# Two weight-folding matmuls and a sparse attention on one core: loads in 1 MB pieces, and batch 0 ahead of the fold

## The chip, the cores and the metric

The kernel runs on one core of a Trainium2 chip. The metric is the device time of one execution in microseconds. The kernel before the change took 296.65 us, the median of 13 runs between 292.83 and 298.26.

The engines are TensorE (PE, with its weight loads PEld), VectorE (DVE), ScalarE (ACT), GpSimd (POOL) and SyncE (SP). Each takes its instructions in the order in which the program was laid out for it. SP issues all loads, ACT issues the stores of the output, POOL makes most of the casts from fp32 to fp16.

## The reference

```python
# 8 batches, 8 heads, 576 tokens, head size 64
scores = (q @ k.T) / 8
mask_local   = (rel >= 0) & (rel < 32)                    # heads 0 to 3
mask_strided = (rel >= 0) & (col % 32 == row % 32)        # heads 4 to 7
x = softmax(where(mask, scores, -1e9)) @ v                # to (4608, 512)
a, b = x @ w1, x @ w2                                     # 512 -> 1024
out = ((a * b) @ w3) @ w_out                              # 1024 -> 1024 -> 512
```

Inputs and output are fp32: q, k and v of 9.4 MB each, w1, w2 and w_out of 2 MB, w3 of 4 MB; the output has 9.4 MB.

## The kernel before

**Fold.** No nonlinear step stands between w3 and w_out, so the kernel first computes w34 = w3 @ w_out (1024 x 512) once. For each of 8 row blocks of w3, `fold_tr` transposes the fp16 block on TensorE and copies the result to `w3T` (one half by DVE, one by ACT), and `fold_mm` multiplies it with `woh`, the fp16 w_out, in two halves of four matmuls, the second of which evicts the sum to `w34`. The row blocks in fp16 (`w3n`) have four buffers.

**Attention.** Each batch has four pairs of heads: two local, two strided. A pair goes through the steps `ph_T` (transposes of q and k, copied from PSUM to `qT`, `kT`), `ph_S` (scores, then exp on ACT to `pte` and the product with a mask on DVE to `ptm`), `ph_PV` (twice: product with v, reciprocal of the sums, and the scaled product `xqs`) and `ph_T2` (transposes of the result, copied to `xT`). `ph_R`, once a batch, transposes the last 64 tokens of q and k. The scores and the PV results share a PSUM pool of two buffers (`psB`), the transposes have a pool of one (`psM`). In batches 0 and 1 (`b < AHEAD`) ACT makes all copies of `ph_T` and `ph_R`; later DVE makes those of k.

**Feed-forward.** The 4608 tokens are taken in 9 chunks of 512. `ab_halves` gives 16 units (8 for a, 8 for b; four matmuls of 512 columns each; ACT copies a out of PSUM, DVE multiplies it with b to `abt`). `o_halves` gives 8 units with w34, and stores four blocks of output.

**Order.** It is written out by hand. All attention steps stand in one list, `stream`. `host(units, upto, lead)` lays out units one after the other and, after each, as many steps of the list as bring it evenly to `upto`. `pe(...)` holds the matmuls in this order. Before, the fold hosts batch 0, ab of chunk 0 hosts 8 steps of batch 1 (the first nine units none), o of chunk 0 the other 17, and each later chunk hosts the next batch. Stream steps run one batch ahead of the chunk that needs them.

**Loads.** Each `load_*` helper takes a staging buffer from `stgp` (nine of 0.5 MB), issues DMAs on SP and casts on POOL (w1 on ACT). A batch has q and k in two groups of four heads (packets of 1 KB), their last 64 tokens (`load_rest`, 256 B), local v (`load_vL`, 256 B) to partitions 32 to 127, from where DVE copies to the low ones, and strided v (`load_vS`, 2 KB). A load waits for its staging buffer's last cast, and a cast for the buffer that it writes. The weights are mixed with batch 0: w3 and w_out first, then w1 and w2 in quarters, then batch 1.

Of the kernel before, what the change touches and what calls it, by code (L numbers as in the profile page):

```python
# [8 lines left out]
FP32 = mybir.dt.float32  # L9
FP16 = mybir.dt.float16  # L10
# [4 lines left out]
def _ap(t: bass.AP, off_add, dims):  # L15
    return bass.AP(tensor=t.tensor, offset=t.offset + off_add, ap=dims)
# [3 lines left out]
def kernel(  # L20
# [27 lines left out]
    LQ, LT = 96, 6  # L48
# [3 lines left out]
    KW = 640  # L52

    consts = ctx.enter_context(tc.tile_pool(name="consts", bufs=1))
    stgp = ctx.enter_context(tc.tile_pool(name="stgp", bufs=9))
    qkp = ctx.enter_context(tc.tile_pool(name="qkp", bufs=2))
    att = ctx.enter_context(tc.tile_pool(name="att", bufs=2))
    ffn = ctx.enter_context(tc.tile_pool(name="ffn", bufs=2))
# [6 lines left out]
    def pe(ins):  # L65
        return tc.keep_in_program_order(ins)

    def copy(eng, out, in_):
        if eng == "a":
            nc.scalar.copy(out=out, in_=in_)  # L70
        elif eng == "v":
            nc.vector.tensor_copy(out=out, in_=in_)  # L72
        else:
            nc.gpsimd.tensor_copy(out=out, in_=in_)  # L74
# [55 lines left out]
    w3T = [ffn.tile([P, KF // 2, DF], FP16, tag="abt", bufs=4, name=f"w3T{i}") for i in range(2)]  # L130
    w3n = {}

    def load_wo(g, eng):
        src = moe_w_out.rearrange("(c p) n -> p c n", p=P)
        st = stgp.tile([P, 2, DM], FP32, tag="stg")
        nc.sync.dma_start(st, src[:, 2 * g:2 * g + 2, :])
        copy(eng, woh[:, 2 * g:2 * g + 2, :], st)

    def load_w3(jc, eng):
        st = stgp.tile([P, DF], FP32, tag="stg")  # L140
        nc.sync.dma_start(st, moe_w3[bass.ds(jc * P, P), :])
        t = ffn.tile([P, DF], FP16, tag="w3n", bufs=4)
        w3n[jc] = t
        copy(eng, t, st)

    def load_w12(g):
        cs = bass.ds(g * 256, 256)
        for wd, wh, eng in ((moe_w1, w1h, "a"), (moe_w2, w2h, "p")):
            st = stgp.tile([P, KM, 256], FP32, tag="stg")
            nc.sync.dma_start(st, wd.rearrange("(c p) n -> p c n", p=P)[:, :, cs])  # L150
            copy(eng, wh[:, :, cs], st)


    x16 = {}

    def load_qk(b, grp, engs="pp"):
        for nm, ten, eng in (("q", q, engs[0]), ("k", k, engs[1])):
            st = stgp.tile([P, 4, 4, D], FP32, tag="stg")
            nc.sync.dma_start(st.rearrange("p h c d -> p h (c d)"),
                              ten[b, 4 * grp:4 * grp + 4, 0:NM].rearrange("h (p c) d -> p h (c d)", c=4))  # L160
            t = qkp.tile([P, 4, 4, D], FP16, tag=f"{nm}{grp}")
            copy(eng, t, st.rearrange("p h c d -> p c h d"))
            x16[(b, nm, grp)] = t

    def load_rest(b, eng="p"):
        st = stgp.tile([P, H, D], FP32, tag="stg")
        for i, ten in enumerate((q, k)):
            nc.sync.dma_start(st[64 * i:64 * i + 64], ten[b, :, NM:S].rearrange("h p d -> p h d"))
        t = qkp.tile([P, H, D], FP16, tag="r")
        copy(eng, t, st)  # L170
        x16[(b, "r")] = t

    def load_vL(b):
        vt = v16L[b % 2]
        for hp in range(2):
            hs = slice(2 * hp, 2 * hp + 2)
            st = stgp.tile([P, 2, LT, D], FP32, tag="stg")
            for h in range(2):
                nc.sync.dma_start(st[32:P, h], v[b, 2 * hp + h].rearrange("(t p) d -> p t d", p=LQ))  # L179
            for pr in (bass.ds(32, 32), bass.ds(64, 64)):  # L180
                nc.gpsimd.tensor_copy(out=vt[pr, hs, :, 0:D], in_=st[pr])  # L181
            nc.vector.tensor_copy(out=vt[0:32, hs, 1:LT, 0:D], in_=vt[96:P, hs, 0:LT - 1, 0:D])

    def load_vS(b):
        vt = v16S[b % 2]
        for hp in range(2):
            st = stgp.tile([SQ, 2, ST, D], FP32, tag="stg")
            sf = st.rearrange("p h c d -> p h (c d)")
            sv = v[b, 4 + 2 * hp:6 + 2 * hp].rearrange("h (p c) d -> p h (c d)", c=ST)
            nc.sync.dma_start(sf[0:64], sv[0:64])  # L190
            nc.sync.dma_start(sf[64:SQ], sv[64:SQ])
            nc.gpsimd.tensor_copy(out=vt[:, 2 * hp:2 * hp + 2, :, 0:D], in_=st)  # L192


    class Pair:
# [101 lines left out]
    def ab_halves(tch):  # L297
        tok = bass.ds(tch * NT, NT)
        res = []

        def first():
            abts[tch] = ffn.tile([P, KF, NT], FP16, tag="abt", bufs=4, name=f"abt{tch}")

        for jc in range(KF):
            st = {}

            def a(jc=jc, st=st):
                if jc == 0:
                    first()
                aps = psF.tile([P, NT], FP32, tag="f")  # L310
                for ci in range(KM):
                    pe(nc.tensor.matmul(aps, w1h[:, ci, bass.ds(jc * P, P)], xT[ci][:, tok],  # L312
                                        start=(ci == 0), stop=(ci == KM - 1)))
# [12 lines left out]
        return res  # L326
# [84 lines left out]
    load_w3(0, "p")  # L411
    for g in range(4):
        load_wo(g, "p")
    load_w3(1, "p")
    load_qk(0, 0)
    load_rest(0)
    load_w3(2, "p")
    load_vL(0)
    load_w3(3, "p")
    load_qk(0, 1)  # L420
    load_w3(4, "p")
    load_w3(5, "p")
    load_vS(0)
    load_w3(6, "p")
    load_w3(7, "p")
    load_w12(0)
    load_w12(1)
    load_w12(2)
    load_qk(1, 0)
    load_rest(1)  # L430
    load_w12(3)
    load_vL(1)
    load_qk(1, 1)
    load_vS(1)

    fold = []
    fold_tr(0)
# [6 lines left out]
    host(fold, batch_end[0], lead=3)  # L444
    load_qk(2, 0)
    load_rest(2)
    load_vL(2)
    host(ab_halves(0), pos[0] + 8, lead=9)
    load_qk(2, 1)
    load_vS(2)  # L450
    host(o_halves(0), batch_end[1])
    for tch in range(1, NTILE):
        units = ab_halves(tch) + o_halves(tch)
        if tch + 1 < B:
            more = tch + 2 < B
            if more:
                load_qk(tch + 2, 0)
                load_rest(tch + 2)
                load_vL(tch + 2)
            mid = (pos[0] + batch_end[tch + 1]) // 2  # L460
            host(units[0:12], mid)
            if more:
                load_qk(tch + 2, 1)
                load_vS(tch + 2)
            host(units[12:], batch_end[tch + 1])
        else:
            for u in units:
                u()
# [30 lines left out]
```

The softmax here doesn't subtract the row's maximum and nothing guards it: scores larger than these inputs give would overflow.

## Time and profile before

| What | Value |
|---|---|
| Median of 13 runs | 296.65 us |
| The profiled execution | 297.62 us, its span 295.9 us |
| Busy in the span: PE, PEld, DVE, ACT, POOL | 268.2, 141.9, 169.9, 146.7, 102.3 us |
| DMA | 48.64 MB, 163 GB/s over the span |
| Bytes moved, 14 to 22 us and 22 to 30 us | 181 and 344 GB/s |
| Cast of 128 x 1024 on POOL, on ACT | 1074 (median 1040), 1048 ns |
| exp of 128 x 576, of 72 x 576 on ACT | 657, 644 ns |
| mask product on DVE, local, strided | 612, 571 ns |
| reciprocal and product on DVE, local | 182 + 554 ns |
| reciprocal and product on DVE, strided | 199 + 685 ns |

The busy times are shares of the whole span; the matmuls' own times overlap, since they are pipelined. The execution falls into three parts: a head of some 84 us, in which the weights and the first batches come in, six stages of 28 us (a chunk hosting a batch each), and two chunks without attention of 20.7 us each at the end.

### The profile page before, as it was taken

To read this page: it belongs to the slowest core of one execution; us is meant where nothing else is said; L and a number is where in the kernel's file an instruction comes from. 1 tells how busy PE (TensorE), PEld (TensorE's weight loads), DVE (VectorE), ACT (ScalarE), POOL (GpSimd) and SP (SyncE) were. 2 spreads that over 40 slices of the span, in tenths; PEclk is the share of its full clock that TensorE was granted. 3 is DMA by queue.
4 is the path that set the end of the run, shared out by engine and by line. 5 is a ranking of instruction groups with operands and counts; after the bars stand their busy time and mean duration, and the time that the engine had idled before them with its cause. 6 is when DMAs were issued, how large, how long until landed. Compare 5 with 4: busy or idle time off the path is not lost.

```text
span 295.9 us, 6132 instructions
## 1 busy us (share of the span) xinstructions
PE 268.2 (91%) x2401; PEld 141.9 (48%) x2401; DVE 169.9 (57%) x353; ACT 146.7 (50%) x269; POOL 102.3 (35%) x118
## 2 busy tenths in 40 slices
PE   2349998987979999999999999999999999999995
PEld 1115554444545555555555455555554555444442
DVE  2012864364878865896788479657755774330420
ACT  2025596556655465546554644555465545323332
POOL 5638643366746634753456435110000000000000
PEclk9986999999999999999999999999999999999999
DMA  7999999899969948995997692120021002003003
GB/s 235 360 180 352 290 348 243 158 252 212 293 205 231 271 114 256 277 167 181 270 232 198 201 278 45 38 106 2 2 73 73 0 2 106 35 2 134 8 2 142
DMA packets 58653, 48.64 MB, mean 164 GB/s; under 512 B 29184, under 2 KB 49664, under 8 KB 58624
## 3 DMA queue, kind: packets, MB, share of 16 engines
q1 hardware_dynamic: 53440, 38.81, 54.5%
q10 hardware_dynamic: 5184, 9.44, 8.8%
q8 instruction: 19, 0.31, 0.5%
q14 instruction: 10, 0.08, 0.1%
HBM read 38.80 MB, written 9.44 MB: 163 GB/s over the span
## 4 chain that ended last, share of the span: by engine, by line
PE 64%; DMA 21%; ACT 5%; DVE 2%; issue 2%; SPq 2%; POOL 1%; ACTq 0%
PE bps L321 18%; PE ops L335 18%; PE aps L312 17%; DMA st<-in_moe_w_dram 10%; DMA st<-in_k_dram 6%; PE xps L268 4%; PE ps L214 3%; DMA st<-in_moe_w_out_dram 3%; DMA out_dram<-osb 3%; PE sps L248 2%; ACT pte L253 2%; PE ps L284 2%; ACT xT L291 1%; SPq L179 1%; ACT osb L346 1%
## 5 line engine op out<-in xcount | busy, mean ns | idle before, releaser
L312 PE MATMUL aps<-xT,w1h 128*128 128x512 f16 x288 | 75.3, 379 | 2.5 <-ACT xT L291 2.4
L323 DVE TENSOR_TENSOR abt<-bps,asb 128x512 f16<-128x512 f32 x72 | 49.5, 687 | 47.1 <-PE bps L321 45.4
L321 PE MATMUL bps<-xT,w2h 128*128 128x512 f16 x288 | 74.0, 379 | 0.0
L315 ACT COPY asb<-aps 128x512 f32<-128x512 f32 x72 | 42.2, 586 | 63.9 <-PE aps L312 61.1
L335 PE MATMUL ops<-w,abt 128*128 128x512 f16 x288 | 71.5, 379 | 0.0
L74 POOL CAST t<-st 128x1024 f16<-128x1024 f32 (+1 forms) x48 | 47.7, 998 | 37.9 <-DMA st<-in_k_dram 24.6
L253 ACT ACTIVATE pte<-sps 128x576 f16<-128x576 f32 (+1 forms) x64 | 38.4, 650 | 8.2 <-PE sps L248 7.1
L276 DVE TENSOR_TENSOR xqs<-xps,rcp 96x384 f16<-96x384 f32 (+1 forms) x64 | 39.6, 619 | 2.0
L321 PEld LDWEIGHTS <-w2h 128*128 128x128 f16 x288 | 25.8, 97 | 30.9 <-issue 4.8
L70 ACT COPY qT<-ps 128x512 f16<-128x512 f16 (+1 forms) x48 | 22.9, 481 | 29.0 <-PE ps L214 22.6
L312 PEld LDWEIGHTS <-w1h 128*128 128x128 f16 x288 | 25.1, 98 | 22.2
L335 PEld LDWEIGHTS <-abt 128*128 128x128 f16 x288 | 24.7, 98 | 22.2
L346 ACT COPY osb<-ops 128x512 f32<-128x512 f32 x36 | 21.1, 586 | 27.7 <-PE ops L335 27.7
L181 POOL CAST v16L<-st 32x768 f16<-32x768 f32 (+1 forms) x32 | 26.9, 840 | 20.0 <-PE xps L268 10.7
L268 PEld LDWEIGHTS <-ptm 72*128 72x128 f16 (+1 forms) x448 | 21.6, 97 | 18.3 <-DVE ptm L255 5.7
L255 DVE TENSOR_TENSOR ptm<-pte,maskL 128x576 f16<-128x576 f16 x32 | 19.4, 612 | 12.8 <-ACT pte L253 12.3
L72 DVE COPY kT<-ps 128x512 f16<-128x512 f16 (+1 forms) x36 | 18.8, 535 | 9.7 <-ACT qT L70 9.6
L192 POOL CAST v16S<-st 72x1024 f16<-72x1024 f32 x16 | 17.1, 1074 | 20.6 <-PE xps L268 12.9
L255 DVE TENSOR_TENSOR ptm<-pte,maskS 72x576 f16<-72x576 f16 x32 | 18.1, 571 | 8.4 <-ACT pte L253 7.8
L335 PE MATMUL ops<-woh,w3T 128*128 128x512 f16 x64 | 19.8, 439 | 2.2 <-POOL woh L74 1.5
L214 PEld LDWEIGHTS <-t 128*128 128x128 f16 x256 | 17.1, 99 | 9.3 <-issue 2.6
L214 PE MATMUL ps<-id,t 128*128 128x128 f16 x256 | 20.3, 222 | 0.8 <-POOL t L74 0.8
(48 smaller groups left out, 173.2 us busy)
## 6 DMA issues: line engine op xcount, KB each, us to landing
out_dram<-osb ACTq DMA_DIRECT2D x36, 256.0 KB, 2.0
st<-in_moe_w_dram SPq DMA_DIRECT2D x16, 512.0 KB, 9.4
st<-in_q_dram SPq DMA_DIRECT2D x16, 512.0 KB, 5.4
st<-in_k_dram SPq DMA_DIRECT2D x16, 512.0 KB, 5.7
st<-in_v_dram SPq DMA_DIRECT2D x32, 144.0 KB, 5.7
st<-in_v_dram SPq DMA_DIRECT2D x16, 256.0 KB, 7.6
st<-in_moe_w_out_dram SPq DMA_DIRECT2D x4, 512.0 KB, 7.4
st<-in_q_dram SPq DMA_DIRECT2D x8, 128.0 KB, 7.1
```

Of the source, the lines that this page charges most:

```text
L74: nc.gpsimd.tensor_copy(out=out, in_=in_)
L181: nc.gpsimd.tensor_copy(out=vt[pr, hs, :, 0:D], in_=st[pr])
L214: pe(nc.tensor.transpose(ps[:, i, c * P:(c + 1) * P], src[:, c, h0:h0 + 2].rearrange("p h d -> p (h d)"), id16))
L253: nc.scalar.activation(out=pte[0:kr], in_=sps[0:kr, :, 0:288], func=AF.Exp, bias=0.0, scale=scale)
L255: nc.vector.tensor_mul(ptm[0:kr, 0:576].rearrange("p (a x) -> p a x", x=w), pte[0:kr].rearrange("p h (a x) -> p (h a) x", x=w), _ap(mk, 0, ...
L268: pe(nc.tensor.matmul(xps[:, h, i * 65:(i + 1) * 65], ptm[0:kr, c0:c0 + P], vt[0:kr, 2 * (s.hp % 2) + h, g * m + i, :], start=True, stop=T ...
L276: nc.vector.tensor_mul(xqs[0:w, 0:m].rearrange("p i h d -> p h i d"), xv[:, :, :, 0:D], _ap(rcp, 0, [[rp, w], [4, 2], [1, m], [0, D]]))
L312: pe(nc.tensor.matmul(aps, w1h[:, ci, bass.ds(jc * P, P)], xT[ci][:, tok], start=(ci == 0), stop=(ci == KM - 1)))
L315: nc.scalar.copy(out=asb, in_=aps)
L321: pe(nc.tensor.matmul(bps, w2h[:, ci, bass.ds(jc * P, P)], xT[ci][:, tok], start=(ci == 0), stop=(ci == KM - 1)))
L323: nc.vector.tensor_mul(abts[tch][:, jc, :], bps, st["asb"])
L335: pe(nc.tensor.matmul(st["ps"], lhs(ci), rhs(ci), start=(ci == 0), stop=(ci == KF - 1)))
```

## The change

- The staging pool has five buffers of 1 MB in place of nine of 0.5 MB; `load_rest` has a buffer of its own.
- q and k of all heads come in one DMA each, local v in one, strided v in one of 64 partitions and one of 8; w1 and w2 come in halves of 512 columns, w_out in halves, w3 in four pairs of row blocks. Casts keep their sizes, except local v's, of which there are two per batch in place of four. Of each half of w_out one cast is on POOL and one on ACT; of batch 0, k's casts are on ACT; of w3, the second row block's.
- Order of the loads: batch 0, w1 and w2, the first pair of w3, w_out, the rest of w3, batch 1.
- The stream's steps of batch 0 stand alone, each after a `spin`: two matmuls of the identity whose result nobody reads.
- Then ab of chunk 0 and 8 of the 24 fold units without stream steps, then the other 16 fold units and o of chunk 0 as hosts of batch 1.
- Later chunks host their batch evenly in one piece, and all loads of a batch stand before the chunk.

```diff
-    stgp = ctx.enter_context(tc.tile_pool(name="stgp", bufs=9))
+    stgp = ctx.enter_context(tc.tile_pool(name="stgp", bufs=5))
...
+    def load_wo(g):
+        st = stgp.tile([P, 4, DM], FP32, tag="stg")
+        nc.sync.dma_start(st, src[:, 4 * g:4 * g + 4, :])
+        for i, eng in enumerate("pa"):
+            copy(eng, woh[:, 4 * g + 2 * i:4 * g + 2 * i + 2, :], st[:, 2 * i:2 * i + 2, :])
+
+    def load_w3(g, engs="pp"):
+        src = moe_w3.rearrange("(c p) n -> p c n", p=P)
+        st = stgp.tile([P, 2, DF], FP32, tag="stg")
         nc.sync.dma_start(st, src[:, 2 * g:2 * g + 2, :])
+        for i in range(2):
+            t = ffn.tile([P, DF], FP16, tag="w3n", bufs=4)
+            w3n[2 * g + i] = t
+            copy(engs[i], t, st[:, i])
...
     def load_w12(g):
         for wd, wh, eng in ((moe_w1, w1h, "a"), (moe_w2, w2h, "p")):
+            st = stgp.tile([P, KM, 512], FP32, tag="stg")
+            nc.sync.dma_start(st, wd.rearrange("(c p) n -> p c n", p=P)[:, :, bass.ds(g * 512, 512)])
+            for i in range(2):
+                copy(eng, wh[:, :, bass.ds(g * 512 + i * 256, 256)], st[:, :, bass.ds(i * 256, 256)])
...
+    def load_qk(b, engs="pp"):
+            st = stgp.tile([P, H, 4, D], FP32, tag="stg")
+                              ten[b, :, 0:NM].rearrange("h (p c) d -> p h (c d)", c=4))
...
     def load_vL(b):
+        st = stgp.tile([P, 4 * LT, D], FP32, tag="stg")
+        nc.sync.dma_start(st[32:P], v[b, 0:4].rearrange("h (t p) d -> p (h t) d", p=LQ))
+        for pr in (bass.ds(32, 32), bass.ds(64, 64)):
+            nc.gpsimd.tensor_copy(out=vt[pr, :, :, 0:D], in_=st[pr].rearrange("p (h t) d -> p h t d", t=LT))
+        nc.vector.tensor_copy(out=vt[0:32, :, 1:LT, 0:D], in_=vt[96:P, :, 0:LT - 1, 0:D])
...
+    def spin():
+        ps = psF.tile([P, NT], FP32, tag="f", name="spin")
+        for i in range(2):
+            pe(nc.tensor.matmul(ps, id16, _ap(id16, 0, [[id16.ap[0][0], P], [0, 4], [1, P]]),
+                                start=True, stop=True))
+
+    load_qk(0, "pa")
     load_rest(0)
     load_vL(0)
     load_vS(0)
     load_w12(0)
     load_w12(1)
+    load_w3(0, "pa")
+    for g in range(2):
+        load_wo(g)
+    for g in range(1, 4):
+        load_w3(g)
+    load_qk(1)
     load_rest(1)
     load_vL(1)
     load_vS(1)
...
+    fold = [lambda: fold_tr(0)]
...
+    ALONE = batch_end[0]
+    host([spin] * ALONE, ALONE)
+    load_qk(2)
     load_rest(2)
     load_vL(2)
     load_vS(2)
+    host(ab_halves(0) + fold[0:8], pos[0])
+    host(fold[8:] + o_halves(0), batch_end[1])
...
+            host(units, batch_end[tch + 1])
```

More of the change, by code (lines that the diff above doesn't have):

```diff
@@ L131 @@
     w3n = {}
-    def load_wo(g, eng):
+    def load_wo(g):
         src = moe_w_out.rearrange("(c p) n -> p c n", p=P)
-        st = stgp.tile([P, 2, DM], FP32, tag="stg")
-        nc.sync.dma_start(st, src[:, 2 * g:2 * g + 2, :])
[L137 to L144, printed above, removed]
+        st = stgp.tile([P, 4, DM], FP32, tag="stg")
+        nc.sync.dma_start(st, src[:, 4 * g:4 * g + 4, :])
+        for i, eng in enumerate("pa"):
+            copy(eng, woh[:, 4 * g + 2 * i:4 * g + 2 * i + 2, :], st[:, 2 * i:2 * i + 2, :])
@@ L146, in load_w12 @@
+    def load_w3(g, engs="pp"):
+        src = moe_w3.rearrange("(c p) n -> p c n", p=P)
+        st = stgp.tile([P, 2, DF], FP32, tag="stg")
+        nc.sync.dma_start(st, src[:, 2 * g:2 * g + 2, :])
+        for i in range(2):
+            t = ffn.tile([P, DF], FP16, tag="w3n", bufs=4)
+            w3n[2 * g + i] = t
+            copy(engs[i], t, st[:, i])
     def load_w12(g):
-        cs = bass.ds(g * 256, 256)
         for wd, wh, eng in ((moe_w1, w1h, "a"), (moe_w2, w2h, "p")):
-            st = stgp.tile([P, KM, 256], FP32, tag="stg")
-            nc.sync.dma_start(st, wd.rearrange("(c p) n -> p c n", p=P)[:, :, cs])
-            copy(eng, wh[:, :, cs], st)
+            st = stgp.tile([P, KM, 512], FP32, tag="stg")
+            nc.sync.dma_start(st, wd.rearrange("(c p) n -> p c n", p=P)[:, :, bass.ds(g * 512, 512)])
+            for i in range(2):
+                copy(eng, wh[:, :, bass.ds(g * 512 + i * 256, 256)], st[:, :, bass.ds(i * 256, 256)])
@@ L154 @@
     x16 = {}
-    def load_qk(b, grp, engs="pp"):
-        for nm, ten, eng in (("q", q, engs[0]), ("k", k, engs[1])):
-            st = stgp.tile([P, 4, 4, D], FP32, tag="stg")
+    def load_qk(b, engs="pp"):
+        sts = {}
+        for nm, ten in (("q", q), ("k", k)):
+            st = stgp.tile([P, H, 4, D], FP32, tag="stg")
             nc.sync.dma_start(st.rearrange("p h c d -> p h (c d)"),
[L160 to L163, printed above, removed]
@@ L165, in load_rest @@
-    def load_rest(b, eng="p"):
-        st = stgp.tile([P, H, D], FP32, tag="stg")
+                              ten[b, :, 0:NM].rearrange("h (p c) d -> p h (c d)", c=4))
+            sts[nm] = st
+        for grp in range(2):
+            for nm, eng in zip("qk", engs):
+                t = qkp.tile([P, 4, 4, D], FP16, tag=f"{nm}{grp}")
+                copy(eng, t, sts[nm][:, 4 * grp:4 * grp + 4].rearrange("p h c d -> p c h d"))
+                x16[(b, nm, grp)] = t
+    def load_rest(b):
+        st = stgp.tile([P, H, D], FP32, tag="rst", bufs=1)
@@ L169, in load_rest @@
         t = qkp.tile([P, H, D], FP16, tag="r")
-        copy(eng, t, st)
+        nc.gpsimd.tensor_copy(out=t, in_=st)
         x16[(b, "r")] = t
@@ L174, in load_vL @@
         vt = v16L[b % 2]
[L175 to L182, printed above, removed]
+        st = stgp.tile([P, 4 * LT, D], FP32, tag="stg")
[3 more added lines that the diff above has]
+        nc.vector.tensor_copy(out=vt[0:32, :, 1:LT, 0:D], in_=vt[96:P, :, 0:LT - 1, 0:D])
     def load_vS(b):
         vt = v16S[b % 2]
[L186 to L192, printed above, removed]
+        st = stgp.tile([SQ, 4, ST, D], FP32, tag="stg")
+        sf = st.rearrange("p h c d -> p h (c d)")
+        sv = v[b, 4:8].rearrange("h (p c) d -> p h (c d)", c=ST)
+        nc.sync.dma_start(sf[0:64], sv[0:64])
+        nc.sync.dma_start(sf[64:SQ], sv[64:SQ])
+        for i in range(2):
+            nc.gpsimd.tensor_copy(out=vt[:, 2 * i:2 * i + 2, :, 0:D], in_=st[:, 2 * i:2 * i + 2])
     class Pair:
@@ L408, in host @@
                 pos[0] += 1
[L411 to L415, printed above, removed]
+    def spin():
+        ps = psF.tile([P, NT], FP32, tag="f", name="spin")
+        for i in range(2):
+            pe(nc.tensor.matmul(ps, id16, _ap(id16, 0, [[id16.ap[0][0], P], [0, 4], [1, P]]),
+                                start=True, stop=True))
+    load_qk(0, "pa")
     load_rest(0)
-    load_w3(2, "p")
     load_vL(0)
[L419 to L422, printed above, removed]
     load_vS(0)
-    load_w3(6, "p")
-    load_w3(7, "p")
     load_w12(0)
     load_w12(1)
-    load_w12(2)
-    load_qk(1, 0)
+    load_w3(0, "pa")
[4 more added lines that the diff above has]
+    load_qk(1)
     load_rest(1)
-    load_w12(3)
     load_vL(1)
-    load_qk(1, 1)
     load_vS(1)
-    fold = []
-    fold_tr(0)
+    fold = [lambda: fold_tr(0)]
     for jc in range(KF):
@@ L443 @@
         fold.append(h1)
-    host(fold, batch_end[0], lead=3)
-    load_qk(2, 0)
+    ALONE = batch_end[0]
+    host([spin] * ALONE, ALONE)
+    load_qk(2)
     load_rest(2)
     load_vL(2)
-    host(ab_halves(0), pos[0] + 8, lead=9)
-    load_qk(2, 1)
     load_vS(2)
-    host(o_halves(0), batch_end[1])
+    host(ab_halves(0) + fold[0:8], pos[0])
+    host(fold[8:] + o_halves(0), batch_end[1])
     for tch in range(1, NTILE):
@@ L456 @@
             if more:
-                load_qk(tch + 2, 0)
+                load_qk(tch + 2)
                 load_rest(tch + 2)
                 load_vL(tch + 2)
[L460 to L463, printed above, removed]
                 load_vS(tch + 2)
-            host(units[12:], batch_end[tch + 1])
+            host(units, batch_end[tch + 1])
         else:
```

## The prediction

> **What bounds the kernel now.** I read the strip of 40 slices first, then the busy times by stretch, then the chain of waits, then the timelines of POOL, ACT and PE over the first 85 us.
>
> ```profile
> PE   2349998987979999999999999999999999999995
> ...
> PEclk9986999999999999999999999999999999999999
> DMA  7999999899969948995997692120021002003003
> ```
>
> Each digit is a slice of 7.4 us. TensorE is full from about slice 12 to the end; only the head has holes, and there the DMA engines are full.
>
> ```profile
> 14.00:22.00 8.00, 3.96 (x21) 1.84 (x19) 1.11 (x2) 1.66 (x3) 3.46 (x4) 0.88 1.23 181
> ...
> 40.00:50.00 10.00, 8.66 (x99) 4.88 (x97) 6.28 (x15) 8.45 (x14) 3.63 (x4) 1.00 1.14 297
> ...
> 85.00:113.00 28.00, 27.53 (x272) 14.93 (x272) 20.85 (x44) 15.31 (x29) 13.81 (x15) 1.00 0.93 214
> ...
> 197.00:225.00 28.00, 27.53 (x272) 14.94 (x272) 18.41 (x40) 15.31 (x29) 0.00 (x0) 1.00 0.11 39
> ```
>
> Columns: stretch, length, busy PE, weight loads, DVE, ACT, POOL, clock, DMA share, GB/s. A stage (one token chunk with one batch of attention in it) takes 28.0 us with POOL and DMA at work or without, so nothing but TensorE sets it.
>
> ```profile
> 2.75 7.79 DMA st<-in_moe_w_out_dram
> 10.54 10.53 DMA st<-in_moe_w_dram
> ...
> 57.81 8.30 DMA st<-in_k_dram
> ...
> 264.76 6.91 PE ops L335 x32
> ```
>
> The chain of waits runs through loads up to 66 us and through matmuls from 85 on. The last line gives the price of a unit of four 512-column matmuls: 6.91 / 8 = 0.864 us. A chunk is 16 ab units and 8 o units, 20.7 us; a batch of attention is the other 28.0 - 20.7 = 7.3 us.
>
> ```profile
> 22.60 1.69 POOL L181 CAST v16L<-st 32x768 f16<-32x768 f32 x2 [0.45 <-DMA st<-in_v_dram]
> ...
> 59.28 3.45 POOL L181 CAST v16L<-st 32x768 f16<-32x768 f32 x4 [0.38 <-DMA st<-in_v_dram]
> ...
> 48.25 1.27 PE L312 MATMUL aps<-xT,w1h 128*128 128x512 f16 x4
> ...
> 64.20 0.36 PE L268 MATMUL xps<-v16L,ptm 128*128 128x65 f16 x6 [1.13 <-DVE ptm L255]
> ...
> 83.59 0.81 PE L312 MATMUL aps<-xT,w1h 128*128 128x512 f16 x3
> ...
> 41.98 1.06 ACT L70 CAST w1h<-st 128x1024 f16<-128x1024 f32 x1
> ```
>
> These are the landmarks: chunk 0 starts at 48.25, batch 1's first PV at 64.20, chunk 1 at 83.6. From 83.6 on the same work remains in both kernels, so **the change is worth the shift of the start of chunk 1.**
>
> [...] matmuls of 512 columns came every 0.43 us until 27 us, 0.216 later. [...]
>
> **Price of a load.**
>
> ```profile
> q1 hardware_dynamic: 53440, 38.81, 54.5%
> q10 hardware_dynamic: 5184, 9.44, 8.8%
> ```
>
> q10: 8.8% of 16 x 295.9 us over 5184 packets is 80 ns for 1820 B; q1 gives 48 ns for 726 B. The line through both is 27 ns + 0.0293 ns per byte, an estimate. Spread on 16 engines: q or k of a batch (1024 packets of 1 KB) 3.6 us each, the rests 2.2, local v (2304 of 256 B) 4.9, strided v 1.6: 15.9 us per batch. w1 and w2 in halves with 2 KB rows: 2.8 each, 11.1 in all, against 14.5 in 1 KB rows. w_out 5.6, w3 9.4. Casts start some 4.5 us after the sum of what is ahead: local v of batch 0 in the kernel before has 17.4 (first half) ahead and in it, and its cast starts at 22.6.
>
> **The change part by part.**
>
> 1. Batch 0 first. Sum up to its local v: 3.6 + 3.6 + 2.2 + 4.9 = 14.4, so it lands at 18.9. POOL casts: twice the columns of the two that took 1.69, so 3.3; DVE's copy to the low partitions, 640 columns at 0.32, is doubled, 0.65. First PV at 22.9 (before: 28.95).
>
> 2. Batch 0 alone. Nothing useful stands between its steps, so it is a chain of latencies: S, exp (0.65 each), mask (0.5), PV, reciprocal and product (0.73 local, 0.89 strided), and the next S needs those two PSUM buffers back. PV of both groups, transposes of pair 2 and three spins: S of pair 1 at 25.3. Its exps stand behind two copies on ACT: 26.2 to 27.4, PVs by 28, products by 29.2, S of pair 2 at 29.4. Now the order on ACT matters: both casts of w1's first half (2 x 1.05) stand between the qT and kT copies of pair 3, in front of pair 2's exps: ACT gets to these at 32.2 instead of 30.1. PVs 33.4 and 34.1, products by 35.6, S of pair 3. The casts of w1's second half stand between its two exps: second exp done at 38.2, mask 38.7, PV 39.1, product 40, transposes and xT copy: chunk 0 starts at 40.6 and waits 0.6 for xT. Only 7.3 us of useful work of TensorE were done until then.
>
> 3. Spins: 21 times two matmuls, 0.43 us each warm, 9 us. They run while TensorE waits; the three in step 2 cost about 1.2. At half clock each is 0.86.
>
> 4. ab of chunk 0, unhosted: 16 x 0.864 = 13.8; w1 and w2 are there. Ends at 54.9. ACT has three casts of 1.05 in it, against 8 x (1.73 - 0.59) us free: hidden.
>
> 5. First 8 fold units: five of 0.864, three transposes of 0.45, and about 0.9 for the first w3T copies, 6.6: the fourth transposes are done at 61.5. w3n has four buffers, so POOL's cast of the eighth row block waits for exactly these, and behind it on POOL stand k's casts of batch 1 and everything after. Cast 62.6, k 63.6, transposes of batch 1; k's second 64.7, rest 65.3, local v 3.3 to 68.6, DVE copy: first PV of batch 1 at 69.3.
>
> 6. Staging of five 1 MB buffers in place of nine of 0.5 MB: w_out's first half needs w1's buffer, released by the casts of step 2 at 31.7, wanted by 29.4; w3's last needs the w3 cast on ACT after chunk 0's start. Some 2 us in all: local v of batch 1 lands at 62.9 rather than 60.8. POOL comes to it only at 65.3: covered. Without that cover it would set the PV at 66.9.
>
> 7. After that PV: 8 fold units 6.9, three transposes 1.35, 8 o units 6.9, 7.0 of attention, 0.7 of waits like those seen in other stages: 22.9, so chunk 1 starts at 92.2, 8.6 later than 83.6. Before, 19.4 us followed the PV, with 6 us of holes since only 8 o units covered 17 steps; the new hosting fills these, but with work that was done earlier before.
>
> 8. Later stages: same order of work, loads 15.9 + 2.9 of output per 28 us; batch 2's q and k land near 73, wanted near 83. Nothing, except that POOL's local-v casts become 1.65 us long, and DVE products of two SBUF operands grew from 0.46 to 1.08 beside POOL already: 0 to 1 us in each of 4 stages; I take 0.3 in all. Moving half of w_out's casts to ACT: nothing (step 4). Uniform hosting instead of two halves: nothing.
>
> 9. Clock, not shown by the trace for so sparse a pattern: between 0 (spins hold it) and +5 us (half clock through step 2: three spins and five groups per pair double, about 1.5 per pair). I take 1.
>
> Sum: 8.6 + 0.3 + 1 = +9.9 on the profiled execution (span 295.9, run 297.6): 307.5. That run lies 1 us above the median of 296.65; against the median I say 306.5.
>
> **Rivals.**
> - *Loads alone decide.* If ACT's casts hide and batch 0 is through by 36, the first PV of batch 1 follows its local v without stalls: 60.8 + 3.3 + 0.7 = 64.8, chunk 1 at 87.7, +4.1: 300.7. For it: DMA is full in the whole head. Against: the ACT order above.
> - *Half clock.* Spins don't hold the clock; step 2 grows by 5 and chunk 0 starts cold: +14, 310.5 to 311.5. For it: a burst from 13.5 to 17.8 us in the trace did not raise the clock. Against: step 2 is mostly waits on ACT and DVE.
> - *Faster.* 1 MB pieces move at the 349 GB/s that the stretch from 2 to 14 us (w3 and w_out) shows: batch 0's local v lands at 14.3, 4.6 earlier, and ACT's casts cost nothing (4.2): chunk 0 at 31.8, batch 1's PV at 60.5. The point is 83.6 - 22.9 = 60.7; below it the change gains. With the clock warm throughout it would reach 295. Against: 1 KB and 256 B packets moved at 181 GB/s from 14 to 22 us, and these keep their length.
>
> **How the numbers follow.** Forecast 0.62, loads alone 0.16, half clock 0.16, faster 0.06 (half of it within the bound). A measurement of this kernel can tell 0.5%, 1.5 us. Slower by more than that: 0.93, within 0.04, faster 0.03. The forecast's own range is 303 to 310; taking in both slower rivals it is 300.5 to 313.5.
>
> **What would show it.** First PV of batch 0 near 23 us; the w1 casts inside batch 0's chain on ACT; chunk 0 near 41; TensorE waiting for POOL near 62 to 64; batch 1's first PV near 69; chunk 1 near 92; 28 us stages after. I am wrong if chunk 1 starts before 84, or if the stages after it differ from 28 us by more than 0.5.

## The result, and the profile after

The changed kernel takes 316.96 us, the median of 11 runs (313.05 to 318.86), beside 296.02 us for the kernel before (48 runs). The ratio is 1.0697, with a 95% interval from 1.0661 to 1.0732: slower by 7%. The forecast was 306.5, slower by 3.3%. The profiled execution took 317.12 us, 19.5 more than that of the kernel before (297.62); the sum of the prediction was 9.9. The medians are 20.9 apart, since the profiled execution of the kernel before is one of its slower ones.

The strip of 40 slices of the changed kernel; a slice is now 7.9 us:

```profile
PE   2567799773999999999999899999999999999995
...
POOL 5264230796740663219404340810000000000000
PEclk9989999977899999999999999999999999999999
DMA  7998899899906992899895940011002001102003
```

As before, TensorE is full from about slice 11 on, and the holes are in the head. There is a new one in the ninth and tenth slices (63 to 79 us): TensorE falls to 7 and 3 tenths while GpSimd is at 9 and 6, and the granted clock is at 7 to 8 tenths from 63 to 87 us.

The timeline of the changed kernel (start, duration, engine, line, operation, count, and in brackets the idle time ahead of it with what ended it), first the landmarks on TensorE with two rows of ScalarE:

```profile
20.84 0.38 PE L272 MATMUL xps<-v16L,ptm 128*128 128x65 f16 x4 [2.22 <-DVE v16L L186]
...
28.67 1.99 ACT L70 CAST w1h<-st 128x1024 f16<-128x1024 f32 x2
...
35.30 1.98 ACT L70 CAST w1h<-st 128x1024 f16<-128x1024 f32 x2
...
39.98 1.27 PE L316 MATMUL aps<-xT,w1h 128*128 128x512 f16 x4
...
54.03 0.61 PE L361 MATMUL trp<-id,t 128*128 128x128 f16 x8
...
64.20 0.40 PE L218 MATMUL ps<-id,t 128*128 128x128 f16 x4 [2.56 <-POOL t L74]
...
66.14 1.91 PE L339 MATMUL ops<-woh,w3T 128*128 128x512 f16 x4
...
69.43 1.04 PE L339 MATMUL ops<-woh,w3T 128*128 128x512 f16 x4
...
76.22 0.38 PE L272 MATMUL xps<-v16L,ptm 128*128 128x65 f16 x4 [4.74 <-DVE v16L L186]
...
101.27 0.81 PE L316 MATMUL aps<-xT,w1h 128*128 128x512 f16 x3
```

Chunk 0 starts at 39.98 (before: 48.25), batch 1's PV is complete at 76.22 (64.20; in the changed kernel this is the start of the four matmuls that read the copied rows of v), chunk 1 starts at 101.27 (83.59). So 17.7 of the 19.5 us are there when chunk 1 starts. The early start of chunk 0 isn't a gain, since the fold, which the kernel before had done by then, still lies ahead.

The same timeline between 59 and 77 us, GpSimd and VectorE, shows where the largest part of the surprise lies:

```profile
59.17 5.96 POOL L74 CAST t<-st 128x1024 f16<-128x1024 f32 x6 [1.12 <-PE trp L361]
...
65.75 2.97 POOL L185 CAST v16L<-st 32x1536 f16<-32x1536 f32 x2
68.79 2.02 POOL L196 CAST v16S<-st 72x1024 f16<-72x1024 f32 x2
70.75 4.50 POOL L74 CAST t<-st 128x1024 f16<-128x1024 f32 x4
75.21 0.61 POOL L177 CAST t<-st 128x512 f16<-128x512 f32 x1
...
70.39 0.79 DVE L259 TENSOR_TENSOR ptm<-pte,maskL 128x576 f16<-128x576 f16 x1 [0.79 <-ACT pte L257]
71.42 0.97 DVE L259 TENSOR_TENSOR ptm<-pte,maskL 128x576 f16<-128x576 f16 x1 [0.24 <-ACT pte L257]
72.42 3.74 DVE L186 COPY v16L<-v16L 32x1280 f16<-32x1280 f16 x1
```

Local v of batch 1 is cast by 68.72. VectorE's copy of it to the low partitions has two mask products ahead of it, starts at 72.42, and then lasts 3.74 us: it ends 0.35 us after GpSimd's row of casts, which has no gap of over 0.1 us from 59.17 to 75.82.

Stretches around that, on the same kernel (length, busy PE, weight loads, DVE, ACT, POOL, granted clock, DMA share, GB/s):

```profile
64.00:68.00 4.00, 3.80 (x18) 1.70 (x19) 0.69 (x1) 1.85 (x6) 3.89 (x5) 0.61 1.03 350
...
72.00:76.00 4.00, 0.00 (x0) 0.00 (x0) 3.97 (x2) 0.00 (x0) 3.81 (x5) 0.89 1.09 136
76.00:80.00 4.00, 3.78 (x29) 2.66 (x29) 2.08 (x6) 0.00 (x0) 1.18 (x1) 0.50 1.07 203
80.00:84.00 4.00, 4.00 (x38) 1.97 (x35) 1.69 (x2) 3.08 (x6) 3.77 (x4) 0.75 1.09 346
```

TensorE does nothing from 72 to 76 us, and in the next 4 us its granted clock is 0.50. In the trace's clock records it is 0.50 from 75.1 to 82.0 us. It was 0.50 once before in batch 1, from 64.9 to 68.3 us, after TensorE's wait of 2.56 us for the cast of k: a unit of four matmuls took 1.91 us at 66.14 and 1.04 at 69.43.

The waits of TensorE (for what, us in all, times, longest), changed kernel:

```profile
PE xps L272 <- DVE v16L L186: 7.0, 2, 4.7
PE ps L218 <- POOL t L74: 5.9, 2, 3.3
PE xps L272 <- DVE ptm L259: 4.7, 8, 1.0
PE ps L218 <- ACT t L70: 3.0, 1, 3.0
```

The first row, 7.0 us for VectorE's copies of local v in batches 0 and 1, wasn't among the long waits of the kernel before.

### The profile page after: what moved, and what is told of

The parts are those of the page before. It is cut to its first block, busy times and chain, and to the rows that moved or that the text cites. A ratio compares the mean times of both kernels' runs of the same rounds, so it can differ in the third digit from the quotient of the medians.

```text
span 315.4 us, 6055 instructions
## 1 busy us (share of the span) xinstructions
PE 281.2 (89%) x2443; PEld 146.6 (46%) x2443; DVE 170.8 (54%) x345; ACT 152.0 (48%) x274; POOL 93.5 (30%) x97
## 4 chain that ended last, share of the span: by engine, by line
PE 73%; DVE 9%; ACT 8%; DMA 5%; issue 2%; POOL 1%; SPq 0%; ACTq 0%; POOLq 0%; DVEq 0%
PE ops L339 21%; PE bps L325 19%; PE aps L316 17%; PE ps L218 5%; PE xps L272 4%; ACT pte L257 3%; DVE ptm L259 3%; DMA st<-in_k_dram 3%; PE sps L252 3%; DVE v16L L186 2%; PE spin L419 2%; ACT xT L295 2%; PE ps L288 2%; DVE xqs L280 1%; POOL t L74 1%
## 5 line engine op out<-in xcount | busy, mean ns | idle before, releaser
L339 PE MATMUL ops<-w,abt 128*128 128x512 f16 x288 | 70.7, 379 | 0.0
L74 POOL CAST t<-st 128x1024 f16<-128x1024 f32 x37 | 39.0, 1082 | 43.7 <-PE ps L218 17.9
L259 DVE TENSOR_TENSOR ptm<-pte,maskL 128x576 f16<-128x576 f16 x32 | 18.6, 590 | 23.6 <-ACT pte L257 23.0
L185 POOL CAST v16L<-st 32x1536 f16<-32x1536 f32 (+1 forms) x16 | 23.8, 1490 | 22.3 <-DMA st<-in_v_dram 12.3
L218 PE MATMUL ps<-id,t 128*128 128x128 f16 x256 | 21.8, 232 | 8.9 <-POOL t L74 5.9
L218 PEld LDWEIGHTS <-t 128*128 128x128 f16 x256 | 18.3, 105 | 18.6 <-POOL t L74 7.2
L259 DVE TENSOR_TENSOR ptm<-pte,maskS 72x576 f16<-72x576 f16 x32 | 19.9, 629 | 10.8 <-ACT pte L257 10.6
L196 POOL CAST v16S<-st 72x1024 f16<-72x1024 f32 x16 | 17.1, 1087 | 26.7 <-PE xps L272 19.9
L278 DVE RECIPROCAL rcp<-xps 96x6 f32<-96x6 f32 (+1 forms) x64 | 12.2, 191 | 20.3 <-PE xps L272 20.1
```

The costliest lines, as they stand in the source:

```text
L185: nc.gpsimd.tensor_copy(out=vt[pr, :, :, 0:D], in_=st[pr].rearrange("p (h t) d -> p h t d", t=LT))
L218: pe(nc.tensor.transpose(ps[:, i, c * P:(c + 1) * P], src[:, c, h0:h0 + 2].rearrange("p h d -> p (h d)"), id16))
L259: nc.vector.tensor_mul(ptm[0:kr, 0:576].rearrange("p (a x) -> p a x", x=w), pte[0:kr].rearrange("p h (a x) -> p (h a) x", x=w), _ap(mk, 0, ...
L339: pe(nc.tensor.matmul(st["ps"], lhs(ci), rhs(ci), start=(ci == 0), stop=(ci == KF - 1)))
```

## The experiments

Two theories stood at the start. *Held copy*: batch 1's PV is late because VectorE's copy waits for GpSimd's row of casts. *Late head*: what is lost is lost ahead of the fold, by ScalarE's order, by the spins, or by batch 0's loads.

**e1: the copy on ScalarE**

```diff
-        nc.vector.tensor_copy(out=vt[0:32, :, 1:LT, 0:D], in_=vt[96:P, :, 0:LT - 1, 0:D])
+        nc.scalar.copy(out=vt[0:32, :, 1:LT, 0:D], in_=vt[96:P, :, 0:LT - 1, 0:D])
```

> The copy of local v to the low partitions moves from VectorE to ScalarE; all else keeps its place in the first 100 us, but for the casts of w1's first half, which come one copy earlier on ScalarE. Theory L (that copy on VectorE is held off while GpSimd casts without a break; 3.74 us in place of 0.5): the copy for batch 1 takes about 1.2 us on ScalarE and ends near 72.5, batch 1's first PV is complete near 73 instead of 76.4, TensorE keeps its clock, chunk 1 starts 4 to 7 us earlier (94 to 97), and batch 0's first PV comes 0.5 earlier: time 309 to 312, ratio to before 1.045 to 1.055. Theory O (the order on ScalarE and GpSimd alone makes the delay, the copy only happens to be last): chunk 1 stays within 1.5 us of 101.3, time 315 to 318.

Measured: 311.43 us, ratio 1.049 (1.0381 to 1.06).

```profile
68.68 4.50 POOL L74 CAST t<-st 128x1024 f16<-128x1024 f32 x4
...
69.94 1.26 ACT L186 COPY v16L<-v16L 32x1280 f16<-32x1280 f16 x1
...
71.25 0.38 PE L272 MATMUL xps<-v16L,ptm 128*128 128x65 f16 x4 [1.86 <-ACT v16L L186]
71.44 1.90 PE L339 MATMUL ops<-woh,w3T 128*128 128x512 f16 x4
```

In this kernel's timeline the same copy, on ScalarE, takes 1.26 us beside the same row of casts. PV is complete 5.0 us earlier than in the changed kernel; 2.1 of these are a fold that starts earlier (51.96), the other 2.9 go with the copy. The four matmuls at 71.44 take 1.90 us, as those behind the hole of the changed kernel did (76.41), and the granted clock is 0.83 from 68 to 72 us and 0.74 from 72 to 76: the slow clock isn't avoided.

**e2: the casts of w3's last two row blocks on ScalarE**

```diff
-        load_w3(g)
+        load_w3(g, "aa" if g == 3 else "pp")
```

> The casts of w3's last two row blocks move from GpSimd to ScalarE, so that GpSimd's casts of batch 1 no longer stand behind the fourth fold transposes. If that wait is what holds batch 1 (step 5 of the prediction): k's transposes of batch 1 follow q's without the 2.6 us gap, the casts of local v start near 62 as soon as it has landed, the VectorE copy comes before the casts of batch 2 are ready, first PV of batch 1 at 66 to 68, chunk 1 at 91 to 94, time 307 to 310. If the loads of batch 1 are what is late and the wait only covers them: gap stays over 1.5 us and the time gains less than 3 us (314 to 317).

Measured: 310.81 us, ratio 1.0521 (1.0426 to 1.0616); batch 1's PV complete at 72.46, chunk 1 at 96.35. It gains a little less than expected, although chunk 0 starts 1.6 us later in this execution (41.56), and not in the way expected: TensorE still waits once for 3.5 us for batch 1's q and k. GpSimd's row of casts ends at 71.20; a mask product is held until then (69.08 to 71.51), and the copy behind it takes 0.49 us.

**e3: w1's casts on GpSimd**

```diff
-        for wd, wh, eng in ((moe_w1, w1h, "a"), (moe_w2, w2h, "p")):
+        for wd, wh, eng in ((moe_w1, w1h, "p"), (moe_w2, w2h, "p")):
```

> All casts of w1 move from ScalarE to GpSimd, out of batch 0's chain. By step 2 of the prediction both pairs of casts cost their 2.1 us: chunk 0 starts 3.5 to 4.2 us earlier (36 rather than 40), and if nothing else is late, chunk 1 too: time 312.5 to 313.5. If batch 1's loads then decide, chunk 0 gains 4 but batch 1's first PV less than 2: time 314.5 to 316.5. If the casts were hidden: chunk 0 within 0.5 of 40, time as the changed kernel's 317.

Measured: 311.42 us, ratio 1.0533 (1.0463 to 1.0602). Chunk 0 starts at 37.15, 2.8 us earlier: this is the price of the two pairs of casts in ScalarE's order, less than the 3.5 to 4.2 expected. The rest of the gain comes from batch 1, where the copy took 1.22 us this time.

**e4: no spins**

```diff
-    host([spin] * ALONE, ALONE)
+    host([lambda: None] * ALONE, ALONE)
```

> No spins in batch 0's steps; nothing else changes. If they only fill waits and hold the clock: TensorE runs batch 0 at half clock to the end of its steps, chunk 0 starts 1 to 3 us later and its first units at half clock, time 318 to 322. If they cost and hold nothing: chunk 0 0.5 to 1.5 us earlier, time 315.5 to 316.5.

Measured: 309.72 us, ratio 1.0471 (1.0406 to 1.0536), faster than either theory had it. Chunk 0 starts at 34.85, 5.1 us earlier, though chunk 0 itself takes 16.1 us in place of 14.05, with its first two units at 1.90 and 1.91 us and those from 39.72 on at 1.03. So the spins cost more (up to the 5.1 us) than the rate that they hold (2.05 us in chunk 0). Not all of the 5.1 is theirs: w1's second pair of casts on ScalarE also fell behind both exps of the last pair here, at 32.38, and not between them.

The timeline of e4 in batch 1:

```profile
66.70 2.02 POOL L74 CAST t<-st 128x1024 f16<-128x1024 f32 x2
...
66.06 2.97 DVE L259 TENSOR_TENSOR ptm<-pte,maskL 128x576 f16<-128x576 f16 x1 [0.21 <-ACT pte L257]
69.06 0.49 DVE L186 COPY v16L<-v16L 32x1280 f16<-32x1280 f16 x1
```

Here the mask product is held, to 69.03, 0.31 us after GpSimd's row ended at 68.72; the copy behind it is back at 0.49. So it is not the copy's own slowness: a mask product in its place is held in the same way.

**e5 and e6: the pieces alone, the order alone.** e5 is the kernel before, in its order and hosting, with the loads of the changed kernel:

```diff
-    stgp = ctx.enter_context(tc.tile_pool(name="stgp", bufs=9))
+    stgp = ctx.enter_context(tc.tile_pool(name="stgp", bufs=5))
...
-    load_qk(0, 0)
+    load_qk(0)
     load_rest(0)
-    load_w3(2, "p")
+    load_w3(1)
     load_vL(0)
```

e6 is the changed kernel, with its order, hosting and spins, and the loads of the kernel before:

```diff
-    load_qk(0, "pa")
+    load_qk(0, 0, "pa")
     load_rest(0)
     load_vL(0)
+    load_qk(0, 1, "pa")
     load_vS(0)
-    load_w12(0)
-    load_w12(1)
+    for g in range(4):
+        load_w12(g)
```

> The kernel before, its order of loads and its hosting, with the 1 MB pieces, their casts and the five staging buffers. If the order makes the delay (batch 0 alone on TensorE, then the fold late): within 0.5 to 2% of before, 295 to 302; batch 0's first PV some 4 us later than 28.95, since q and k of all heads now stand ahead of local v, and chunk 1 at 84 to 88. If the pieces make it (longer runs of casts on GpSimd, coarser staging): 306 or more, with a VectorE copy or product of two SBUF operands held for over 2 us in front of batch 1's first PV.

> The changed kernel's order of loads, spins and hosting, with the pieces and nine staging buffers of the kernel before; the casts of w_out alternate between GpSimd and ScalarE, w3's second row block is cast on ScalarE. If the order makes the delay: chunk 0 near 40, chunk 1 at 93 to 101, time 308 to 317. If the pieces make it: chunk 1 before 88, time under 302.

Measured: e5 302.4 us, ratio 1.0291 (1.019 to 1.0391), chunk 1 at 86.83. e6 298.24 us, ratio 1.011 (1.0038 to 1.0182), chunk 1 at 82.46. That the order makes the loss falls: alone it costs 1%, although the fold is left for later in it too. That the pieces alone make it falls too: e5 stays well under 306, and no VectorE copy or mask product in it takes longer than 1.71 us. The parts alone cost 2.9% and 1.1%, together 7%: three of the seven per cent exist only together. In e5 and e6 the number of staging buffers goes with the size of the pieces, so what the five in place of nine cost isn't shown.

The timeline of e6 around batch 1's PV:

```profile
57.48 1.04 POOL L74 CAST t<-st 128x1024 f16<-128x1024 f32 x1
59.56 1.15 POOL L74 CAST t<-st 128x1024 f16<-128x1024 f32 x1 [1.04 <-DMA st<-in_k_dram]
...
59.84 1.05 DVE L182 COPY v16L<-v16L 32x640 f16<-32x640 f16 x1
```

With small pieces, GpSimd's casts wait for loads between one another, and its rows have gaps. The copy, even where it meets a cast, takes 1.05 us.

**e7: e1, e2 and e3 together**

> The edits of the first three experiments in one: copy of local v on ScalarE, casts of w3's last two row blocks on ScalarE, casts of w1 on GpSimd. If each removes a cost of its own: chunk 0 near 35, first PV of batch 1 complete at 64 to 66 (loads of batch 1 decide), chunk 1 at 87 to 90, time 301 to 304. If each only shifts VectorE against the same run of casts on GpSimd, so that one is enough: chunk 1 at 93 to 96, time 307 to 311.

Measured: 305.08 us, ratio 1.0372 (1.0297 to 1.0446), fold at 49.44, PV complete at 65.73, chunk 1 at 89.13. The gains partly add: chunk 1 lies in the first range, the time 1.1 us above it.

**e8: the kernel before, with a third of the fold left for later**

```diff
-    host(fold, batch_end[0], lead=3)
+    host(fold[:16], batch_end[0], lead=3)
...
-    host(o_halves(0), batch_end[1])
+    host(fold[16:] + o_halves(0), batch_end[1])
```

with ab of chunk 0 unhosted.

> The kernel before, with the last 8 of the 24 fold units held back: 16 host batch 0, ab of chunk 0 hosts nothing, and the 8 held units with the 8 o units host all of batch 1. This fills the holes of the head after 64 us (step 7 of the prediction: 6 us) without the loads in another order. If those holes are what is left: chunk 1 at 79 to 82, time 291 to 295. If batch 1's transposes only move later and the holes with them: chunk 1 at 84 to 88, time 296 to 301.

Measured: 302.83 us, ratio 1.0273 (1.0192 to 1.0354), chunk 1 at 87.60: slower than either range. Holding back fold units as cover for batch 1 is a loss in the order of the kernel before too.

**e9: q and k of batch 0 in two groups.** `load_qk0(grp)` loads and casts four heads of q, then of k, in 0.5 MB each; all else stays as in the changed kernel:

```diff
-    load_qk(0, "pa")
+    load_qk0(0)
     load_rest(0)
     load_vL(0)
+    load_qk0(1)
     load_vS(0)
```

> The changed kernel with one thing undone: q and k of batch 0 come in two groups of four heads again (0.5 MB each), with the local values between the groups; all other loads stay in 1 MB pieces. Theory 'late local v' (much of what pieces and order cost only together is that whole q and k stand ahead of batch 0's local v): its casts start some 3.5 us earlier, the first complete PV of batch 0 is at 16.5 to 18 us instead of 20.8, chunk 0 at 36 to 38 instead of 40.0, the fold 2 to 4 us earlier; batch 1's copy on VectorE can still be held, time 308 to 313. Rival 'pieces of the weights' (w1's two casts in a row on ScalarE and the casts in a row on GpSimd decide): chunk 0 moves by less than 1.5 us, time 314 to 317.

Measured: 303.84 us, ratio 1.0278 (1.0236 to 1.0319), 4 us below the lower end of what the theory gave. This one edit takes back 12.0 of the 19.5 us (span 303.4 in place of 315.4). Its timeline:

```profile
14.28 1.04 ACT L70 CAST t<-st 128x1024 f16<-128x1024 f32 x1 [0.44 <-DMA st<-in_k_dram]
...
26.80 2.02 ACT L70 CAST w1h<-st 128x1024 f16<-128x1024 f32 x2
28.69 1.21 ACT L266 ACTIVATE pte<-sps 72x576 f16<-72x576 f32 x2
...
33.66 1.99 ACT L70 CAST w1h<-st 128x1024 f16<-128x1024 f32 x2
...
11.12 2.97 POOL L194 CAST v16L<-st 32x1536 f16<-32x1536 f32 x2 [2.35 <-DMA st<-in_v_dram]
...
60.50 3.11 POOL L194 CAST v16L<-st 32x1536 f16<-32x1536 f32 x2 [2.30 <-DMA st<-in_v_dram]
63.67 2.39 POOL L205 CAST v16S<-st 72x1024 f16<-72x1024 f32 x2
...
63.95 1.22 DVE L195 COPY v16L<-v16L 32x1280 f16<-32x1280 f16 x1
...
16.18 0.38 PE L281 MATMUL xps<-v16L,ptm 128*128 128x65 f16 x4 [1.49 <-DVE v16L L195]
...
32.93 1.27 PE L325 MATMUL aps<-xT,w1h 128*128 128x512 f16 x4
...
65.22 0.28 PE L281 MATMUL xps<-v16L,ptm 128*128 128x65 f16 x4 [1.33 <-DVE v16L L195]
```

Local v comes 3.9 us earlier (its casts start at 11.12, against 15.05 in the changed kernel), PV of batch 0 is complete 4.7 us earlier. Then the gain grows. The order on ScalarE is laid out anew, and w1's two pairs of casts come at 26.80, behind both exps of pair 2, and at 33.66, behind all of batch 0's work; in the changed kernel the first stood in front of pair 2's exps and the second between those of pair 3. Chunk 0 starts 7.1 us earlier. Then it grows again: local v of batch 1 is no longer behind other casts in GpSimd's queue (it waits 2.30 us for its load), and the copy comes through after one cast. PV of batch 1 is complete 11.0 us earlier, chunk 1 11.9. The runs don't separate how much of the last step is luck in where the copy meets the casts.

**e10: batch 2's q and k casts on ScalarE**

```diff
-    load_qk(2)
+    load_qk(2, "aa")
```

> The changed kernel with the four casts of batch 2's q and k on ScalarE instead of GpSimd; VectorE's copy of local v stays where it is. Theory 'held until GpSimd's row of casts ends': that row now ends at 70.8 us or soon after instead of 75.8, VectorE's copy of batch 1's local v ends by 72 (0.5 to 1 us long instead of 3.74), batch 1's PVs are complete at 71.5 to 73 instead of 76.2, chunk 1 at 96 to 98 instead of 101.3, time 311 to 314. Rival 'the copy is late by itself' (its own size, or what VectorE has ahead of it): the copy ends later than 75, PVs at 75 to 77, time at least 315.5.

Measured: 313.55 us, ratio 1.0641 (1.0579 to 1.0702), chunk 1 at 96.78.

```profile
67.59 2.25 POOL L196 CAST v16S<-st 72x1024 f16<-72x1024 f32 x2
73.09 0.61 POOL L177 CAST t<-st 128x512 f16<-128x512 f32 x1 [3.25 <-DMA st<-in_k_dram]
...
69.15 1.00 DVE L259 TENSOR_TENSOR ptm<-pte,maskL 128x576 f16<-128x576 f16 x1 [0.21 <-ACT pte L257]
70.18 0.49 DVE L186 COPY v16L<-v16L 32x1280 f16<-32x1280 f16 x1
...
70.73 0.28 PE L272 MATMUL xps<-v16L,ptm 128*128 128x65 f16 x4 [1.50 <-DVE v16L L186]
70.85 1.02 PE L339 MATMUL ops<-woh,w3T 128*128 128x512 f16 x4
```

This is the plainest test of the held copy: it stays on VectorE, at the same place and size, and only the casts beside it are gone. It takes 0.49 us instead of 3.74, PV is complete 5.5 us earlier (1.2 of it from an earlier fold), and the four matmuls behind it take 1.02 us, not 1.90. The rival, that the copy is late by itself, falls. In the profiled executions the span is 5.2 us shorter (310.2 against 315.4), in the medians 3.4, and the interval of the ratio overlaps the changed kernel's, so the time alone would not have shown it. The four casts on ScalarE have a cost of their own, since they now stand before its other work: a new wait of TensorE, 2.21 us at 82.39 for ScalarE's copies of k.

**e11 and e12: could the new order win?** e6 without its spins, and the same with w1's casts on GpSimd (the edits of e4 and e3):

> The new order with the old 0.5 MB pieces (e6), without the 21 spins. Theory 'spins only take TensorE's time': batch 0 is through 1 to 3 us earlier (chunk 0 at 26 to 28 instead of 29.0) and the time is 294 to 297.5. Rival 'spins hold the clock': the granted clock stays low in batch 0 and in the first units of chunk 0, chunk 0 takes longer than 15 us, time 298.5 to 302.

> As e11 (new order, 0.5 MB pieces, no spins), and w1's four casts on GpSimd, so that ScalarE has only attention's work and k's casts in batch 0. Theory 'ScalarE's order': another 0.5 to 2 us earlier at chunk 0 than e11, time 292.5 to 296.5, level with the kernel before the change or faster. Rival 'GpSimd is then late': w1 or the casts of w3 come later, or VectorE is held more, time 297 to 301.

Measured: e11 299.14 us, ratio 1.0107 (1.007 to 1.0144); e12 298.88 us, 1.0121 (1.0079 to 1.0163). The first units of chunk 0 in e11:

```profile
30.44 1.90 PE L312 MATMUL aps<-xT,w1h 128*128 128x512 f16 x4
...
33.84 1.57 PE L312 MATMUL aps<-xT,w1h 128*128 128x512 f16 x4
35.25 1.03 PE L321 MATMUL bps<-xT,w2h 128*128 128x512 f16 x4
```

The first two units take 1.90 and 1.91 us, against 1.03 from 35.25 on, and chunk 0 starts at 30.44, not at 26 to 28, and takes 16.7 us (15.1 in e6, with spins), as the rival had it: here the rate that the spins hold is worth as much as the time that they take, and what e4 gained is not gained again. Taking w1 off ScalarE brings nothing more that can be measured. No version was faster than the kernel before; the nearest are e6, e11 and e12, all about 1% slower.

## Why the prediction was wrong in size

The direction held, and so did the course of the head up to the fourth transposes of w3; the size was half. By the landmarks of the forecast:

| Landmark (us) | Predicted | Measured |
|---|---|---|
| batch 0's PV (step 1) | 22.9 | 20.84 |
| chunk 0 (step 2) | 40.6 | 39.98 |
| fold (step 4) | 54.9 | 54.03 |
| fourth transposes of w3 (step 5) | 61.5 | 61.2 |
| batch 1's local v cast (step 5) | 68.6 | 68.72 |
| batch 1's PV complete (step 5) | 69.3 | 76.22 |
| from there to chunk 1 (step 7) | 22.9 | 25.05 |
| rest after chunk 1's start, more than before (step 8) | 0.3 | 1.8 |

**The step that failed is the end of step 5**, "local v 3.3 to 68.6, DVE copy: first PV of batch 1 at 69.3": the copy, doubled to 0.65 in step 1, was put right behind the casts of local v. It is 6.9 us off. From the timeline: the first PV matmuls, which wait for a mask product alone, started at 71.24, so 1.9 us are the scores, which came later between the hosted fold units than I had them. The half clock from 64.9 to 68.3 us is most of that: the units at 64.43, 66.14 and 67.85 took 1.45, 1.91 and 0.84 us, where others of their form take 1.03, 1.03 and 0.61, some 1.5 us more in all (an estimate). The wait ahead of it is the one for GpSimd that step 5 did foresee, but with no price for the clock. From 71.24 to 76.22 it is 5.0: 3.25 by which the copy of 3.74 exceeds its unheld 0.49, and 1.7 for the second mask product ahead of it and the copy itself.

In the kernel before the same copy, in two parts of 32x640, had never taken more than 0.995 us, and I took its price from there without asking what its engine had in front of it and what GpSimd would run beside it. e10 shows that the casts beside the copy hold it (0.49 without them, 3.74 with them), and for longer than one of them lasts: three more casts started and ended within the 3.74 us. By what means they hold it, the runs don't show. In step 8 I had seen the sign of it, mask products growing from 0.46 to 1.08 beside GpSimd, and used it only for the later stages.

**Step 9, the clock,** failed too, in its place. I took 1 us, put it into batch 0's chain, and gave a range to 5. The landmarks up to the fold leave no room for it. It came after the two holes in batch 1: in step 5 (the 1.5 us above), and after the held copy, from 75.1 to 82.0 us. There the units at 76.41 and 80.13 took 1.90 and 1.91 us in place of 1.03, and the transposes at 78.44 and 79.28 took 1.04 and 1.06 in place of 0.61: some 2.6 us, an estimate from these durations, which is enough for the 2.15 us more than step 7 gave up to chunk 1. With the 1 us allowed, 1.15 are missing. I had also misread the clock in the kernel before. The burst from 13.5 us on did end at full rate: its last matmuls, at 16.75 and 16.96, took 0.38 us in place of 0.63, and the trace grants 1.00 from 16.6 to 20.0 us and 0.50 from there to 26.9, with a wait of 4.07 us for a cast up to 22.21. So a hole with half clock behind it stood in the trace of the kernel before.

**Step 8, later stages,** was priced too low: 1.8 us more from chunk 1's start to the end, in place of 0.3. The first stage takes 29.03 us and the third 29.48 (before: 28.37 and 27.87), so the prediction's own sign of being wrong, a stage more than 0.5 off 28 us, came true. In the third, two mask products beside the casts of local v take 1.64 and 1.11 us, and TensorE waits 0.8 us for them, which is the mechanism that step 8 named. e1, with the copy on ScalarE, has nearly the same in sum (310.3 - 96.27 = 214.0, before 295.9 - 83.59 = 212.3), spread over four stages of 28.5 to 28.6. e6 (212.1) and e5 (211.0) don't have it, e12, with small pieces, has most of it (213.8). What makes the rest stays open. Sum of the misses: 6.92 + 1.15 + 1.52 = 9.6, the difference of 19.5 and 9.9.

**Steps 1 to 3** came out at chunk 0 to within 0.6 us, but by two errors that cancel. The casts of local v start at 15.05, not 18.9: the 4.5 us that the price of a load adds to the sum of 14.4 were 0.65 (and its own example, 22.6 - 17.4, gives 5.2). The copy then stood behind two mask products, took 1.22 in place of 0.65, beside the casts of strided v, and the chain from PV to chunk 0 took 19.1 us, not 17.7. The casts of w1 stood where the prediction had them, and ScalarE took them in the order laid out, on which step 2 rests (the pair at 28.67 between the copies to qT at 28.19 and to kT at 30.56, the pair at 35.30 between the exps at 34.75 and 37.18). The spins, which step 3 let cost 1.2 up to pair 1, cost more: up to 5 us in all by e4.

**Steps 4 and 6** were right: ScalarE's casts in chunk 0 cost nothing, and batch 1's local v had landed when GpSimd came to it.

**The rivals.** *Loads alone* falls, since batch 1's PV was not set by its load, although e9 shows that the time at which loads arrive in batch 0 was worth more than I gave it. *Half clock* had the nearest number, 310.5 to 311.5, for a wrong reason: from 23.9 us on a spin took 0.6 us, not 1.06, and chunk 0's second unit 1.02, so from there on the clock was held, and removing the spins made the kernel faster. *Faster* was near with local v (14.3, measured 15.05), since the loads moved 325 GB/s from 2 to 8 us and 199 from 8 to 16; it falls with the chain behind it, which ended at 39.98, not 31.8.

**Where the 19.5 us come from**, then: whole q and k of batch 0 ahead of its local v, with all that follows, 12.0 (e9). The other large pieces, in the new order, make 8.8, the difference between the spans of e9 and e6. The order with small pieces ends 1.3 us under the span of the kernel before in the profiled executions, although its ratio over the runs is 1.011: 12.0 + 8.8 - 1.3 = 19.5. What part of the 12.0 is the held copy isn't separate from it: e10 shows some 4 us at batch 1's PV, and e9 loses the hold on its way.

## What to carry to other kernels

The size of a load piece also sets the order in which casts stand on their engines: here the larger pieces brought local v of batch 0 to its casts at 15.05 us, against 11.12 with q and k in two groups, and left GpSimd's row of casts from 59.17 to 75.82 us without a gap of over 0.1 us, and what stood in front of what then decided by several microseconds (12.0 of the 19.5 by e9). Price a small VectorE operation by what is ahead of it in its queue and by the length of GpSimd's row of work beside it, not by its usual duration alone (here 3.74 us beside the row, 0.49 without it). Price a hole in TensorE's work with the stretch behind it too: here 4.7 us without a matmul had half clock behind them, up to 82.0 us, while one of 2.56 us had it in the changed kernel and not in e10. When changes to loads and to order are made together, run each alone: here 2.9% and 1.1% gave 7%.

## What the runs showed of the hardware

- A VectorE operation between SBUF operands that meets a row of GpSimd casts can be held for several of them; those that read TensorE's results kept their length in the same row (0.69 us at 65.92, 0.42 at 69.17 in the changed kernel, where their means are 0.69 and 0.42). In three places the held operation ended 0.31 to 0.35 us after the end of one: after three more casts than the one under way in the changed kernel (copy of 3.74 us), after two more in e4 (mask product of 2.97), after the one under way alone in e9 (copy of 1.22). What decides whether it gets in between two casts wasn't found.
- The same copy of 32x1280 took 0.49 us on VectorE alone and 1.26 on ScalarE, there without a hold.
- The rate of the matmuls follows the granted clock where the trace records it: in the changed kernel four matmuls of 512 columns take 1.91 us at 66.14, under a record of 0.50, and 1.04 at 69.43, under one of 1.00; a spin takes 1.04 us at 21.02, under a record of 0.50 (20.5 to 23.9 us), and 0.61 at 24.81, under one of 1.00 (23.9 to 64.9 us). The 1.00 that the view by stretches gives ahead of the first record, at 17.1 us, is no measurement: a spin took 1.06 us at 15.11. In e11 that view gives 1.00 from 24 to 40 us, while a unit took 1.90 at 30.44 and 1.03 at 35.25.
- In the changed kernel a wait of TensorE of 2.56 us for a cast (61.6 to 64.2 us) and one of 4.74 us for the copy (71.5 to 76.2) went with a granted clock of 0.50, from 64.9 to 68.3 and from 75.1 to 82.0 us; in the kernel before one of 4.07 us (up to 22.21), with 0.50 from 20.0 to 26.9. In e10 a wait of 2.56 us, up to 63.01, had a unit of 1.03 us behind it: the length of the wait alone doesn't decide it, and what does wasn't found.
